# The zeros ahead of the attention's values: a DMA from a constant instead of GpSimd's memset

## The chip, the core and the metric

The kernel runs on one core of one Trainium2 chip. The metric is device time in microseconds (us) of one execution. The core's engines run side by side and meet at semaphores: PE (TensorE, matmuls), DVE (VectorE), ACT (ScalarE), POOL (GpSimd) and SP (SyncE, which only issues DMAs here). POOL and ACT can issue DMAs too.

## What is computed

A sequence of 2048 positions with 512 channels goes through four layers, each added to its input: a state-space convolution (A), a sliding dilated attention (B), then A and B again with the same weights. Cut to what matters:

```python
def _B_ref(x, wqkv, wo):
    H = 32; Dh = D // H
    W, dil = 8, 2
    q, k, v = qkv[0], qkv[1], qkv[2]          # of x @ wqkv
    idx = pos[:, None] - off[None, :]         # off = arange(W) * dil
    mask = idx >= 0
    vg = v[:, :, idx_c, :].reshape(B, H, S, W, Dh)
    logits = jnp.where(mask[None, None, :, :], logits, -1e9)
    attn = _softmax(logits, axis=-1)
    o = jnp.einsum("bhsw,bhswd->bhsd", attn, vg)
    return (lambda x, *d: x.transpose(*d))(o, 0, 2, 1, 3).reshape(B, S, D) @ wo

x = A_u
x = x + _A_ref(_layernorm(x, axis=-1), ...)   # y = causal convolution with a kernel made of A, B, C, dt
x = x + _B_ref(_layernorm(x, axis=-1), B_wqkv, B_wo)
x = x + _A_ref(_layernorm(x, axis=-1), ...)
x = x + _B_ref(_layernorm(x, axis=-1), B_wqkv, B_wo)
```

Each position looks at itself and at the seven positions 2, 4, ... 14 before it. The first positions would look ahead of the sequence's start; there the mask takes the weight away.

## The kernel before

**Layout.** Position 16 p + j lies in partition p at place j, so a partition holds 16 neighbouring positions (`NJ = 16`), and the activations `X` stay in SBUF as 128 partitions × 16 places × 512 channels, in two halves of 256.

**The tile VX.** The attention's values lie in `VX`, of 128 partitions × 2 halves × 30 places × 256 channels in bf16. Places 14 to 29 (`NV = 14`) are the partition's own positions, written by ACT (line 1485). Places 0 to 13 are the 14 positions before them, which belong to the partition one below; the function `shift` copies them there by DMAs of SP from partitions 0 to 126 to partitions 1 to 127 (line 1498). For partition 0 there is nothing to copy: its places 0 to 13, which head the sequence, must hold zeros, so that the products of line 1695 multiply the masked weights with numbers. They are written once, ahead of the first attention layer, and stay for the second.

**The order of the work.** Within a layer the code only declares operations, each with an engine: `pl.op("G", ...)` is for POOL, "V" for DVE, "A" for ACT, "P" for PE and "S" for SP. A written-out list of numbers for each layer (`ORDERS`) sets the order in which they are recorded, and each engine runs its instructions in that order, one after the other. Semaphores are put in by what an instruction reads and writes. So an instruction that stands still holds up all that follow it on its engine, whatever those read.

Constants for the later layers are loaded by POOL's own DMA queue just before the first attention layer; the zeros follow on the same engine:

```python
for name, arr, dt in (("IC2", _bf(C["IC2"]), BF), ("minus", _bf(-np.eye(128)), BF), ("down", np.eye(128, k=1, dtype=np.float32), F32)):
    C[name] = load_const(nc, const2, name, arr, dt, nc.gpsimd)
```

**What runs beside it.** POOL comes to these lines while the other engines are still in the last quarter of the first convolution, in `kernel_and_first_conv`. The channels come in four groups (`dc`), each in four parts. For a part of the kernel's spectrum, PE transposes a stage `Z` (tile `pt`, line 908), DVE copies it to SBUF (`zt`, line 912; other parts go by a transposing DMA of SP, line 885), PE multiplies it (`xp`, line 892) and ACT casts the result (`sp_k`, line 903), which SP also stores to HBM (line 951). For the input's spectrum `sp_u` the two halves of the partitions are also needed swapped; this is done by two DVE copies of 64 partitions each (line 959):

```python
for h in range(2):
    move(box["U"][64 * h:64 * h + 64, t], box["U"][64 - 64 * h:128 - 64 * h, s])
```

DVE then multiplies the spectra (`pa`, line 967), PE transforms back (`vp`, line 981), ACT or DVE casts that to SBUF (`VT`, line 984), and PE forms the output and adds the input (`ps_y`, lines 1000 and 1003), which ACT casts into `X` (line 1007). PE's results lie in three PSUM buffers of one ring (`psA`), used in turn. Then the attention layer begins: PE transposes `X` (`pt_x`, line 1301) and projects it (`ps_qk`, lines 1420 and 1439; `ps_v`, line 1474). DVE multiplies queries with keys (`prod`, line 1519), which PE sums into logits (`Lp`, line 1530).

Of the kernel before, what the change touches and what calls it, by code (L numbers as in the profile page):

```python
# [17 lines left out]
NPBF = ml_dtypes.bfloat16  # L18
# [14 lines left out]
NV = 14  # L33
# [1219 lines left out]
def b_layer(nc, tc, C, X, Wt, VX, XT, pst, eps, ln, center, evac, done, VSTAT_Q):  # L1253

    with ExitStack() as es:
# [19 lines left out]
        pl = Plan(psA=2, psL=1, psO=2, prod=4, LT=3, sm1=1, sm2=1, sm_m=1, sm_s=1, rdb=1)  # L1275
        turned, Kd, Qd, Kx, Vd, Ld, Sd, Od, Rs, Wd, Wl = {}, {}, {}, {}, {}, {}, {}, {}, {}, {}, {}
# [7 lines left out]
        def fetch(name):  # L1284
            if name == "wo":
                for ft in range(4):
                    nc.sync.dma_start(wo_t[:, ft, :], Wt["osrc"][ft])
            else:
                nc.sync.dma_start(bones[:], Wt["bsrc"])
# [523 lines left out]
            done(pl, qt, es)  # L1813

        if center:
            Wl["VX"] = pl.op("G", 1.0, lambda: nc.gpsimd.memset(VX[0:1, :, 0:NV], 0.0))
            for name, us in (("bones", 0.4), ("wo", 2.5)):
                Wl[name] = pl.op("S", us, lambda name=name: fetch(name), lag=5.0)
            for name in "kqv":
                Wd[name] = pl.outer(("w", name))  # L1820
# [39 lines left out]
def kernel(  # L1860
# [38 lines left out]
    with tc.tile_pool(name="mid", bufs=1) as mid:  # L1899
# [38 lines left out]
        def stored(pl, q, after):  # L1938
            for j, a in enumerate(after, q * 4):
                pl.op("S", 0.45, lambda j=j: nc.sync.dma_start(ov[:, j, :].rearrange("p (h c) -> p h c", h=2), X[:, :, j, :]), a, lag=2.2)  # L1940
        b_layer(nc, tc, C, X, Wt, VX, turned_view(U), pst, eps, ln, True, summed, normed, BN_Q)
        a_layer(nc, tc, C, X, kt_dram, U)
        b_layer(nc, tc, C, X, Wt, VX, turned_view(U), pst, eps, ln, False, lambda j, ps: nc.scalar.copy(X[:, :, j, :], halves(ps)), stored, range(4))


# [28 lines left out]
```

## Time and profile before

| | |
|---|---|
| three runs | 439.0, 437.52 and 435.03 us, median 437.52 |
| the profiled execution | 438.79 us, its span 437.0 |
| mean granted clock of PE in it | 0.960 |
| busy in the span | DVE 408.2 us, PE 376.1, ACT 321.1, POOL 33.5 |
| DMA | 51.48 MB, 118 GB/s on average |

The span runs from the first to the last instruction of the profiled execution, and all times of its rows count from the span's start. The granted clock is the share of PE's full clock that the chip's throttle let through. A row that names a line gives an engine's start and duration there; in square brackets stands how long the engine had been idle before it, and what released it. The chain that ended last is followed back from the last instruction: at each step to what released it, or to the instruction before it on its engine.

### The profile page before, as it was taken

To read this page: it belongs to the slowest core of one execution; us is meant where nothing else is said; L and a number is where in the kernel's file an instruction comes from. 1 tells how busy PE (TensorE), PEld (TensorE's weight loads), DVE (VectorE), ACT (ScalarE), POOL (GpSimd) and SP (SyncE) were. 2 spreads that over 40 slices of the span, in tenths; PEclk is the share of its full clock that TensorE was granted. 3 is DMA by queue.
4 is the path that set the end of the run, shared out by engine and by line. 5 is a ranking of instruction groups with operands and counts; after the bars stand their busy time and mean duration, and the time that the engine had idled before them with its cause. 6 is when DMAs were issued, how large, how long until landed. Compare 5 with 4: busy or idle time off the path is not lost.

```text
span 437.0 us, 11576 instructions
## 1 busy us (share of the span) xinstructions
PE 376.1 (86%) x4797; PEld 238.0 (54%) x4834; DVE 408.2 (93%) x682; ACT 321.1 (73%) x524; POOL 33.5 (8%) x97
## 2 busy tenths in 40 slices
PE   1278868898998678999999799899999999998995
PEld 1153646776887565446654345578774346743452
DVE  6999999998999977999899999999999899999994
ACT  6999989998998545667943568999966578853431
POOL 1000000000000700000100240020000010000150
PEclk9757989998999969999999999999999999999999
DMA  8996266777987628000322399089973000223295
GB/s 226 209 281 239 82 97 140 152 154 167 169 140 138 149 67 172 14 18 20 86 85 48 74 232 185 17 152 212 182 125 33 37 1 2 85 83 72 43 157 163
DMA packets 102171, 51.48 MB, mean 118 GB/s; under 512 B 81821, under 2 KB 93998, under 8 KB 101862
## 3 DMA queue, kind: packets, MB, share of 16 engines
q1 hardware_dynamic: 98758, 45.24, 48.4%
q0 software_dynamic: 3072, 5.23, 6.1%
q8 instruction: 38, 0.62, 0.6%
q10 hardware_dynamic: 288, 0.26, 0.2%
q14 instruction: 15, 0.12, 0.1%
HBM read 19.29 MB, written 6.29 MB: 59 GB/s over the span
## 4 chain that ended last, share of the span: by engine, by line
PE 49%; DVE 18%; ACT 10%; issue 4%; DMA 1%; SPq 0%; DVEq 0%; ACTq 0%
PE po L1711 7%; PE ps_v L1474 6%; PE ps_qk L1420 6%; PE ps_qk L1439 6%; DVE prod L1695 5%; PE ps_o L1795 4%; PE Lp L1530 4%; PE ps_s L872 3%; DVE prod L1519 2%; PE psk L483 2%; DVE sp_u L959 2%; PE ps_s L1117 2%; PE vp L981 1%; PE vp L1183 1%; ACT X L1209 1%
## 5 line engine op out<-in xcount | busy, mean ns | idle before, releaser
L1695 DVE TENSOR_TENSOR prod<-VX,L 128x512 bf16<-128x512 bf16 (+2 forms) x72 | 75.4, 1099 | 1.8 <-ACT VX L1485 1.0
L1519 DVE TENSOR_TENSOR prod<-qT,kT 128x4096 bf16<-128x4096 bf16 (+1 forms) x40 | 72.1, 1859 | 2.2 <-ACT kT L1462 1.0
L1711 PE MATMUL po<-prod,sb_ident 128*128 128x512 bf16 x233 | 56.4, 379 | 2.8 <-DVE prod L1695 2.0
L1711 PEld LDWEIGHTS <-sb_ident 128*128 128x128 bf16 x240 | 23.1, 97 | 31.3 <-issue 4.1
L875 ACT CAST Z<-ps_s 128x1024 bf16<-128x1024 f32 (+1 forms) x36 | 31.9, 929 | 1.7 <-PE ps_s L872 1.6
L1474 PE MATMUL ps_v<-wv,U 128*128 128x256 bf16 x256 | 31.4, 273 | 0.6 <-ACT VX L1485 0.3
L1795 PE MATMUL ps_o<-wo_t,oT 128*128 128x512 bf16 x124 | 31.3, 379 | 0.3 <-ACT oT L1744 0.2
L1420 PE MATMUL ps_qk<-U,wqk 128*128 128x512 bf16 x128 | 30.7, 380 | 0.3 <-ACT L L1658 0.3
L1485 ACT ACTIVATE VX<-ps_v,rs 128x256 bf16<-128x256 f32 x64 | 26.7, 473 | 5.6 <-PE ps_v L1474 5.1
L1729 ACT CAST ot<-po 128x1024 bf16<-128x1024 f32 (+1 forms) x16 | 15.1, 958 | 21.2 <-PE po L1711 21.2
L1439 PE MATMUL ps_qk<-U,wqk 128*128 128x512 bf16 x128 | 29.3, 379 | 0.0
L1474 PEld LDWEIGHTS <-U 128*128 128x128 bf16 x256 | 24.3, 97 | 8.9 <-issue 3.1
L1530 PE MATMUL Lp<-prod,sb_bones 128*32 128x512 bf16 x256 | 22.9, 383 | 3.0 <-DVE prod L1519 2.9
L892 PE MATMUL xp<-zt,sb_C 128*128 128x512 bf16 x45 | 16.1, 407 | 8.7 <-DVE zt L912 4.6
L967 DVE TENSOR_TENSOR pa<-sp_u,sp_k 128x2048 bf16<-128x2048 bf16 x16 | 19.4, 1220 | 3.7 <-PE vp L981 2.0
L1359 DVE BATCH_NORM_STATS2 pst<-X 128x6 f32<-128x256 bf16 x64 | 21.8, 407 | 0.5 <-ACT X L1209 0.5
L903 ACT CAST sp_k<-xp 128x1024 bf16<-128x1024 f32 x16 | 16.5, 1041 | 6.9 <-PE xp L892 6.3
L1420 PEld LDWEIGHTS <-wqk 128*128 128x128 bf16 x128 | 11.8, 98 | 16.8 <-issue 3.6
L1439 PEld LDWEIGHTS <-wqk 128*128 128x128 bf16 x128 | 12.2, 98 | 15.4 <-issue 1.6
L1795 PEld LDWEIGHTS <-oT 128*128 128x128 bf16 x128 | 12.2, 98 | 14.7 <-ACT oT L1744 0.7
L872 PE MATMUL ps_s<-KT,FK 128*128 128x128 bf16 (+1 forms) x360 | 18.8, 209 | 1.6 <-ACT KT L845 0.7
L1171 DVE TENSOR_TENSOR pa<-xc,Kt 128x2048 bf16<-128x2048 bf16 x16 | 18.9, 1218 | 0.6 <-PE vp L1183 0.3
(230 smaller groups left out, 863.1 us busy)
## 6 DMA issues: line engine op xcount, KB each, us to landing
kt_scratch<-sp_k SPq DMA_DIRECT2D x16, 256.0 KB, 2.7
Kt<-kt_scratch POOLq DMA_DIRECT2D x16, 256.0 KB, 6.7
sp_u<-sp_u SPq DMA_DIRECT2D x18, 128.0 KB, 2.6
X<-in_A_u_dram SPq DMA_DIRECT2D x8, 256.0 KB, 5.3
X<-in_A_u_dram SPq DMA_DIRECT2D x4, 512.0 KB, 5.3
Kt<-kt_scratch SPq DMA_DIRECT2D x8, 256.0 KB, 5.1
out_dram<-X SPq DMA_DIRECT2D x16, 128.0 KB, 2.0
VX<-VX SPq DMA_DIRECT2D x4, 448.0 KB, 3.7
```

Of the source, the lines that this page charges most:

```text
L872: nc.tensor.matmul(ps[:, r, 0:n // 4, jj * 4:(jj + 1) * 4], w, x, start=(k == 0), stop=(k == len(todo) - 1))
L875: nc.scalar.copy(box["Z", kind, dc, b0][:, 0:n // 4, :, jq * 16:(jq + 1) * 16].rearrange("p g r k -> p r g k"), box.pop(("s1", kind, dc, j ...
L1359: nc.vector.bn_stats(pst[:, j, cp, :], X[:, cp, j, :])
L1420: nc.tensor.matmul(ps[:], wqk[:, ct, f0:f0 + 128], XT[:, ct // 2, 4 * s:4 * s + 4, ct % 2, :], start=(ct == 0), stop=(ct == 3))
L1439: nc.tensor.matmul(box[name][:, k * 512:k * 512 + 512], wqk[:, ct, f0:f0 + 128], XT[:, ct // 2, 4 * s:4 * s + 4, ct % 2, :], start=(ct == ...
L1474: nc.tensor.matmul(ps[:, jj].rearrange("p t h d -> p (t h d)"), XT[:, ct // 2, j + jj, ct % 2, :], wv[:, ct, fp * 256:(fp + 1) * 256], sta ...
L1485: nc.scalar.activation(out, ps, ACT.Identity, scale=r)
L1519: nc.vector.tensor_tensor(pr[:], windows(q, 0, 2), windows(kT[fp][:, a:a + n2, col(w):col(w) + 1024], -DIL * 128, 2), ALU.mult)
L1530: nc.tensor.matmul(Lp[r0:r0 + 32, w // 4, :], bones[:, w % 4 + k, :], pr[:, k, f2 - a, hb * 512:(hb + 1) * 512], start=(n == 1 and k == 0) ...
L1695: nc.vector.tensor_tensor(p2[:].rearrange("p w j t d h -> p w (j t) d h"), windows(v, -DIL * 256, taps), l.to_broadcast([128, taps, nj * 2 ...
L1711: nc.tensor.matmul(po[:, c:c + 512], ident[:], p2[:, t, k + j:k + j + 2].rearrange("p j t d h -> p (j t d h)"), start=first, stop=stop)
L1795: nc.tensor.matmul(ps, oT[:, ft // 2, o:o + 128], wo_t[:, ft, :], start=(ft == 0 and not res), stop=(ft == 3))
```

## The change

POOL no longer writes the zeros itself. They stand in HBM as a constant of the program, and POOL issues a DMA that copies them to the same place, partition 0, places 0 to 13 of both halves, 14336 bytes in two runs of 7168:

```diff
         if center:
-            Wl["VX"] = pl.op("G", 1.0, lambda: nc.gpsimd.memset(VX[0:1, :, 0:NV], 0.0))
+            zeros = nc.inline_tensor(np.zeros((1, 2, NV, 256), NPBF), name="c_zeros")
+            Wl["VX"] = pl.op("G", 1.0, lambda: nc.gpsimd.dma_start(VX[0:1, :, 0:NV], zeros.ap()))
```

`center` is true in the first attention layer only. No instruction changes its place. On POOL, between the constants' loads and the first zeros of the softmax's tiles (`RR`):

```order
 L127 DMA sb_minus<-c_minus 128x128
 L127 DMA sb_down<-c_down 128x128
-L1816 MEMSET VX 1x2x3584
+L1817 DMA VX<-c_zeros 1x2x3584
 L1392 MEMSET RR 1x16
 L1392 MEMSET RR 1x32
```

One row has become a DMA. As it takes one of the eight semaphores on which GpSimd's DMAs are counted in turn, each later one moves to the next. On DVE the first product that reads VX, in the first attention layer, gets one wait more (DMASW5, the zeros' own), with the waits of each instruction in brackets:

```order
 L1644 TENSOR_TENSOR L_4014<-L_4014,sm_m 128x1024 [waits DVE_49]
 L1664 TENSOR_TENSOR L_4014<-L_4014,sm_rdb 128x1024 [waits PE_49,Activation_49]
-L1695 TENSOR_TENSOR prod_4629<-VX,L_4014 128x4096 [waits DMAHW5_49,DMAHW6_49,DVE_49,Activation_49]
+L1695 TENSOR_TENSOR prod_4629<-VX,L_4014 128x4096 [waits DMAHW5_49,DMASW5_49,DMAHW6_49,DVE_49,Activation_49]
 L1695 TENSOR_TENSOR prod_4631<-VX,L_4014 128x4096
```

With the memset no such wait stood there; other waits of the program imply its order. Nothing else on DVE moves but line numbers and semaphore numbers.

## The prediction

> **What bounds the kernel now.** I began with the busy shares, then asked for the one instruction that the change touches and for its neighbours on GpSimd (POOL) in order of time.
>
> ```profile
> PE 376.1 (86%) x4797; PEld 238.0 (54%) x4834; DVE 408.2 (93%) x682; ACT 321.1 (73%) x524; POOL 33.5 (8%) x97
> ```
>
> POOL is busy for 8% of the span, so a shorter POOL instruction is worth nothing by itself.
>
> ```profile
> 146.17 0.54 POOL L127 DMA_DIRECT2D sb_down<-c_down  x1
> 146.69 6.27 POOL L1816 MEMSET VX<- 1x7168 bf16 x1
> 189.06 0.93 POOL L1392 MEMSET RR<- 1x16 bf16 x10 [36.10 <-ACT RR L1386]
> ```
>
> The columns are start, duration, engine, line and operation. The memset runs from 146.69 to 152.96 us, and POOL then idles 36.10 us on ScalarE (ACT): nothing on its own queue waits for it. So I looked at what the other engines did meanwhile, in the list of the copies of line 959 and in the chain that ended last.
>
> ```profile
> L959 DVE COPY sp_u<-sp_u x14: 419/422/6276, 74.0 to 156.4; 64x1024 bf16<-64x1024 bf16 x14
> ```
>
> ```profile
> 146.50 0.45 DVE sp_u L959
> 146.96 0.01 issue
> 146.97 6.28 DVE sp_u L959
> ...
> 154.15 0.70 DVE zt L912
> ...
> 158.49 1.71 PE vp L981 x16
> 160.19 0.45 PE xp L892 x2
> ...
> 161.72 1.24 DVE pa L967
> ...
> 163.00 1.08 PE vp L981 x16
> ...
> 165.77 0.21 PE ps_y L1000
> 165.99 0.45 PE ps_y L1003 x8
> ```
>
> Fourteen VectorE (DVE) copies have one shape and a median of 0.422 us; one took 6.276 us. It starts at 146.97, just inside the memset, and ends at 153.25, 0.29 us after it. The copy is on the chain, and TensorE (PE) sits behind it:
>
> ```profile
> 149.49 0.61 PE L908 MATMUL pt<-sb_ident,Z 128*128 128x128 bf16 x8
> 149.94 0.38 PE L892 MATMUL xp<-zt,sb_C 128*128 128x512 bf16 x1
> 154.90 1.03 PE L892 MATMUL xp<-zt,sb_C 128*128 128x512 bf16 x2 [4.58 <-DVE zt L912]
> ```
>
> PE idles 4.58 us for the copy zt, which stands in DVE's queue behind the blocked one. Here **VectorE, held up by the memset, sets the pace**, not DVE's own work. The stretches of the granted clock (PE busy, then PEclk, DMA share and GB/s) show a second cost:
>
> ```profile
> 98.64:102.06 3.42, 1.72 (x18) 1.00 1.07 200
> 102.06:105.47 3.41, 3.25 (x25) 0.50 0.52 137
> 149.84:153.26 3.42, 0.48 (x6) 1.00 0.62 153
> 153.26:156.67 3.41, 1.77 (x8) 0.50 0.00 0
> 156.67:160.08 3.41, 3.41 (x32) 0.50 0.23 82
> ```
>
> After the stretch with PE busy 0.48 of 3.42 us, its clock is at 0.50 for the next two, to 160.08, so the chain's PE work runs at half speed just when it has to catch up.
>
> **The change part by part.** *Removed:* the memset's 6.27 us on POOL, which covers nothing. With it goes the wait of one copy, 6.28 − 0.42 = 5.86 us of DVE time, so the copies ahead of zt, which now starts at 154.15, would be done at 148.3. *What is late next:* zt copies what PE's eight transposes wrote, done at 149.49 + 0.61 = 150.10. So zt starts at 150.13, not then: 4.02 us earlier than 154.15. The other 1.84 us become idle time of DVE. The matmuls on zt follow 0.75 us after its start, as now (154.15 to 154.90), at 150.88. They also need ACT's cast X, since it frees their PSUM buffer:
>
> ```profile
> 149.69 1.01 ACT L1007 CAST X<-ps_y 128x1024 bf16<-128x1024 f32 x1 [0.59 <-PE ps_y L1003]
> 150.61 1.01 ACT L903 CAST sp_k<-xp 128x1024 bf16<-128x1024 f32 x1
> ```
>
> It ends at 150.70, just in time. PE's idle time falls from 4.58 to some 0.5 us, PE is busy for 0.48 + (153.26 − 150.88) = 2.86 us of the stretch that had 0.48, and its clock should stay at 1.00.
>
> *The half clock:* from 154.90 PE works without a break through xp, two ps_y, vp and another xp, 5.74 us to 160.19 + 0.45. At full clock a 512-column matmul takes 0.21 and eight of L1003 0.45 (rows 165.77 and 165.99), sixteen of vp half of 1.71: 0.43 + 1.32 + 0.86 + 0.43 = 3.04 us. That would be 2.7 us more, if PE alone set the pace; so I follow the other engines: DVE's rows behind zt, and the transposed tile that the last xp reads:
>
> ```profile
> 154.75 1.22 DVE L967 TENSOR_TENSOR pa<-sp_u,sp_k 128x2048 bf16<-128x2048 bf16 x1
> 156.00 0.86 DVE L959 COPY sp_u<-sp_u 64x1024 bf16<-64x1024 bf16 x2
> 157.01 1.22 DVE L967 TENSOR_TENSOR pa<-sp_u,sp_k 128x2048 bf16<-128x2048 bf16 x1
> ```
>
> ```profile
> 149.12 1.24 SPq L885 DMA_TRANSPOSE zt<-Z  x1
> ```
>
> ```profile
> zt<-Z SPq DMA_TRANSPOSE x1, 3.1
> ```
>
> - First pa 0.60 after zt's start (as 154.15 to 154.75), 150.73 to 151.95; PE's vp would start at 150.88 + 0.43 + 1.32 = 152.63, so pa is ready.
> - The last xp 0.86 later at 153.49; its tile lands at 149.12 + 3.1 = 152.2, ready.
> - Two copies 1.25 after pa's start (154.75 to 156.00), 151.98 to 152.84. ACT's sp_k follows the one at 150.61 by 0.92, as that follows X, and ends at 152.54. So the second pa starts at 152.87 (157.01 before) and ends at 154.09; its vp takes 154.12 to 155.2.
> - The third pa waits for the first vp and then runs from 154.0. The fourth waits for the second vp, for ACT's sp_k of the last xp (154.1 to 155.1) and for DVE: it starts at 155.2, against 161.72: **6.5 us earlier**.
> - The vp behind it starts at 156.5 in place of 163.00: again 6.5.
>
> From there, every next step waits for this chain (X, its transposes, the projections), the waits between the instructions are the old ones, and everything moves as a block. *Added:* one DMA issue on POOL at 146.69, by sb_down's row 0.54 us. The row before it is the test of what an issue does to a copy: the copy at 146.50 ran beside sb_down's issue in 0.45 us. The bounds are nothing and, if it held a copy for its whole time, 0.54; even then the copies end by 148.8, before 150.10, so I take **0**. Its landing: 14 KB; the nearest row is 16 KB,
>
> ```profile
> sb_block<-c_block POOLq DMA_DIRECT2D x1, 16.0 KB, 3.8
> ```
>
> so at about 150.5 us. The added wait for it stands at the first product that reads VX:
>
> ```profile
> 215.84 4.49 DVE L1695 TENSOR_TENSOR prod<-VX,L 128x4096 bf16<-128x4096 bf16 x2 [1.01 <-ACT VX L1485]
> ```
>
> This would come at 209.3; behind it stand DVE's further products and PE's sums, but the cover is over 58 us. The semaphores of GpSimd's later DMAs shift by one; what these waits name now was issued before the zeros, or is the zeros, far ahead in the program: 0.
>
> Sum: **−6.5 us on the profiled execution**, whose own time is 438.79 (437.0 span and 1.8 around it): 432.3. How long the half clock lasts hangs on where the 3.41 us stretches fall. Here it lasted 160.08 − 154.90 = 5.2 us into the work, since the stretch with 1.77 us of work didn't end it; placed otherwise, it could end up to one stretch sooner, after 1.8. The loss of 6.5 − 4.0 = 2.5 us would then be 0.9, and this execution is above the median. With 4.0 and the middle, 1.7 (an estimate), the median gains 5.7: 437.52 − 5.7 = **431.8**.
>
> The row of the blocked copy, 0.29 us past the memset's end, bears on a rule: the Trainium skill, "SBUF — State Buffer", "Who interferes with whom", has VectorE's two-port copies and GpSimd instructions share one port pair, which the first to issue keeps to its end. The trace agrees. The same section speaks against this change: descriptors of a GpSimd DMA are written through that pair and starve beside such copies. By that the issue would wait till 148.3 at most, the sum would stay, and the row of 0.45 us shows no copy hurt by one.
>
> **The rivals.** *The clock drops all the same.* PE would have to be half idle between 150 and 157. Against it: the pieces above leave PE little idle time; for it, the stretch 98.64 to 102.06 shows that half idle is enough. Then the gain is zt's 4.0 alone: 433.5.
>
> *The drop comes elsewhere.* The whole program behind 163 us slides against the stretches.
>
> ```profile
> 239.16:242.57 3.41, 1.22 (x11) 1.00 0.16 31
> 242.57:245.98 3.41, 2.33 (x32) 1.00 0.25 46
> ```
>
> A stretch that fell on 239.16 to 242.57 would hold 1.22 us of PE work, less than the 1.72 that sufficed at 98.64. The next 2.33 us of work would double: at most +2.3, so 434.1. The kernel before carries the same risk in other executions, hence a small chance. The Trainium skill, "TensorE: Matmul & The Clock Gate", Part 1 (The HAM clock gate), gives the half clock after an idle window of about 3.4 us; by that alone, no drop could come here, and the row of 98.64 differs, which is why I keep this rival.
>
> *The change doesn't free the copy*, because something other than the memset held it: 437.5. The matching ends and the median of 0.422 us speak against it.
>
> *Slower: the zeros go as single elements.* If the DMA were split into 7168 packets,
>
> ```profile
> q1 hardware_dynamic: 98758, 45.24, 48.4%
> ```
>
> at this queue's 0.484 × 16 × 437.0 / 98758 = 0.034 us each, that is 246 us of one DMA engine. On two engines (VX has two rows here) it lands at 147 + 123 = 270, 61 us after 209.3: some 492. It decides as soon as the landing takes over 62 us, with fewer than four engines. Against it: both sides are two runs of 7168 contiguous bytes.
>
> **How the numbers follow.** Main case 0.80; the clock drops all the same 0.06; elsewhere 0.06; copy not freed 0.04; slower 0.04. A 1% change, about what a measurement of this kernel tells from none, is 4.4 us: faster below 433.1. The main case's runs reach from 435.03 − 5.7 = 429.3 to 439.00 − 5.7 = 433.3, so I put 0.08 of its 0.80 within 1%, with the first three rivals: 0.72, 0.24, 0.04. The range goes from the fastest run with the full gain, 435.03 − 6.5 = 428.5, to the slowest with the least, 439.00 − 4.0 = 435.0, which takes in both clock rivals.
>
> **What would show it.** All fourteen copies of line 959 near 0.42 us; zt right behind the last transposes, near 150.1; PE's wait for it under 1 us; a clock of 1.00 from 150 to 165; vp, now 163.00, near 156.5; the first product on VX 6.5 us earlier and released by ACT, not by the zeros. Wrong would be: a copy as long as before beside the DMA's issue, the clock at 0.50 again, or a gain at 163 us that is gone at the end.

## The result and the profile after

Six runs of the changed kernel took 429.95 to 432.12 us, median **430.52**; six of the kernel before, on the same chip, 435.03 to 439.61, median 438.13. The ratio is **0.9844 (95% interval 0.9803 to 0.9886)**, a gain of 1.6%, by the ratio 6.8 us (5.0 to 8.6). Forecast were 431.8 us and a range of 428.5 to 435.0: faster, by the way described, and a little too cautious. (One run of `pieces` below, 495.43 us with a mean clock of 0.746, and one of before beside it, 462.44 us with 0.858, were slow through the whole program and stand in no ratio, so that the profile of `pieces` is read from the same kernel's run `pieces2`.)

The profiled execution took 430.11 us, its span is 428.3 (438.79 and 437.0 before). First the busy times and the granted clock by slices, from the page of the kernel after:

```profile
PE 370.3 (86%) x4797; PEld 233.4 (54%) x4834; DVE 402.2 (94%) x682; ACT 320.9 (75%) x524; POOL 27.7 (6%) x97
...
PEclk9999999999999999999999999999999999999999
```

and the clock's line from the page of before:

```profile
PEclk9757989998999969999999999999999999999999
```

DVE is busy for 6.0 us less (408.2 before), nearly all of it the one blocked copy. PE is busy for 5.8 us less, though its instructions are the same 4797: it ran at full clock throughout, where before shows four dips: two in the first 60 us, one near 103 us and one near 155. Only the last lies where the change is. Keep this apart; it explains why the profiles differ by more than the change is worth.

Now the place of the change, after. POOL in order of time (start, duration, engine, line and operation):

```profile
143.78 0.54 POOL L127 DMA_DIRECT2D sb_down<-c_down  x1
144.30 0.53 POOL L1817 DMA_DIRECT2D VX<-c_zeros  x1
```

The list of line 959 (least, median and greatest duration in ns):

```profile
L959 DVE COPY sp_u<-sp_u x14: 420/422/502, 73.9 to 150.0; 64x1024 bf16<-64x1024 bf16 x14
```

DVE and then PE in order of time:

```profile
143.25 2.70 DVE L959 COPY sp_u<-sp_u 64x1024 bf16<-64x1024 bf16 x6
147.75 0.69 DVE L912 COPY zt<-pt 128x1024 bf16<-128x1024 bf16 x1 [1.80 <-PE pt L908]
...
150.57 3.67 DVE L967 TENSOR_TENSOR pa<-sp_u,sp_k 128x2048 bf16<-128x2048 bf16 x3
```

```profile
147.10 0.61 PE L908 MATMUL pt<-sb_ident,Z 128*128 128x128 bf16 x8
...
148.50 0.61 PE L892 MATMUL xp<-zt,sb_C 128*128 128x512 bf16 x2 [0.57 <-DVE zt L912]
...
154.30 1.07 PE L981 MATMUL vp<-sb_IC,pa 128*128 128x128 bf16 x16 [0.24 <-DVE pa L967]
```

No copy takes longer than 0.502 us, and DVE now idles 1.80 us until PE's transposes are done: the roles are turned round, and DVE waits for PE. PE's own wait for zt is 0.57 us in place of 4.58. Its clock from there, in one stretch (PE busy, PEclk, DMA share, GB/s):

```profile
150.00:165.00 15.00, 12.88 (x145) 1.00 0.76 171
```

**Where the time came from.** Compare starts, before and after, along the program. sb_down's issue on POOL, ahead of the change, already comes 2.39 us earlier (146.17 to 143.78). That is the early clock, and the change has no part in it. At 42 us PE's rows of the two still agree within 0.04 (42.27 and 42.23, line 1022); behind before's half-clock stretch of 57.69 to 61.10 they are 1.35 apart (62.51 and 61.16, line 838), and behind that of 102.06 to 105.47, 2.39 (105.63 and 103.24, line 483). Before's other executions vary in this too, with mean clocks of 0.960 to 0.994. zt comes 6.40 earlier (154.15 to 147.75), 4.01 more. The fourth pa starts at 153.01, against 161.72: 8.71 earlier, 2.31 more. From there it stays: the first product on VX is 8.70 earlier (215.84 to 207.14), and so is the span's end. So the change is worth 4.01 + 2.31 = **6.3 us** in this pair of profiles, and the early clock the other 2.4.

### The profile page after: what moved, and what is told of

Read it like the earlier page. It is cut to its first block, busy times and chain, and to the rows that moved or that the text cites. A ratio compares the mean times of both kernels' runs of the same rounds, so it can differ in the third digit from the quotient of the medians.

```text
span 428.3 us, 11576 instructions
## 1 busy us (share of the span) xinstructions
PE 370.3 (86%) x4797; PEld 233.4 (54%) x4834; DVE 402.2 (94%) x682; ACT 320.9 (75%) x524; POOL 27.7 (6%) x97
## 3 DMA queue, kind: packets, MB, share of 16 engines
q0 software_dynamic: 3104, 5.24, 6.1%
## 4 chain that ended last, share of the span: by engine, by line
PE 48%; DVE 15%; ACT 14%; issue 4%; DMA 1%; ACTq 0%; DVEq 0%
PE po L1711 8%; PE ps_v L1474 7%; PE ps_qk L1420 7%; PE ps_qk L1439 6%; DVE prod L1695 5%; PE ps_o L1795 4%; PE Lp L1530 4%; PE psk L483 3%; DVE prod L1519 3%; ACT Z L875 2%; DVE pa L967 2%; PE ps_s L1117 2%; PE ps_s L872 1%; ACT sp_k L903 1%; PE vp L1183 1%
## 5 line engine op out<-in xcount | busy, mean ns | idle before, releaser
L892 PE MATMUL xp<-zt,sb_C 128*128 128x512 bf16 x45 | 15.0, 380 | 5.0 <-ACT zt L912 2.3
L872 PEld LDWEIGHTS <-FK 128*128 128x128 bf16 x360 | 17.4, 98 | 3.2 <-issue 2.3
```

The source lines that it names most:

```text
L872: nc.tensor.matmul(ps[:, r, 0:n // 4, jj * 4:(jj + 1) * 4], w, x, start=(k == 0), stop=(k == len(todo) - 1))
```

## The experiments

The theory: (1) the copy is held for exactly as long as GpSimd's memset runs; (2) that delays zt, with PE behind it; (3) the idle time halves PE's clock for the catching up, which costs some 2 us more; (4) the DMA that replaces the memset is free. Each run attacks one of these. Undo, half, pieces and later share the runs of before on one chip (median 437.42); warm, double and pieces2 those on another (436.55). In the table, in us and read from each kernel's own profile, the second column is the time that the six copies of line 959 ahead of zt take together, the third runs from the start of the first of them to zt's start, the fifth from zt's start to that of the fourth pa behind it.

| kernel | the six copies | to zt | PE's wait for zt | zt to fourth pa | ratio to before |
|---|---|---|---|---|---|
| before | 8.48 | 8.51 | 4.58 | 7.57 | 1 |
| after | 2.70 | 4.50 | 0.57 | 5.26 | 0.9844 (0.9803–0.9886) |
| undo | 8.48 | 8.51 | 4.58 | 6.72 | 0.9999 (0.9974–1.0024) |
| half | 5.49 | 5.53 | 1.59 | 5.26 | 0.9879 (0.9838–0.9921) |
| pieces2 | 3.55 | 4.50 | 0.35 | 5.89 | pieces: 0.9864 (0.9819–0.9909) |
| later | 2.62 | 4.51 | 0.57 | 5.26 | 0.9849 (0.9806–0.9891) |
| warm | 8.48 | 8.51 | 0.91, fillers ahead | 5.27 | 0.9949 (0.9930–0.9968) |
| double | 14.34 | 14.36 | 10.22 | 6.53 | 1.0147 (1.0119–1.0175) |

**undo: the DMA stays, a memset of the old size comes back** ahead of it, on places that line 1498 fills later anyway (against after):

```diff
+ nc.gpsimd.memset(VX[32:33, :, 0:NV], 0.0)
  nc.gpsimd.dma_start(VX[0:1, :, 0:NV], zeros.ap())
```

> The changed kernel, with a GpSimd memset of the same size put back ahead of the zeros' DMA; it writes 7168 zeros to partition 32 of VX, which the shift DMAs overwrite later, so the computation is the reference's. Theory A (a memset on GpSimd holds a VectorE copy for as long as it runs): one copy of line 959 takes about 6.3 us and ends some 0.3 us after the memset, TensorE waits about 4.6 us for zt, its clock drops for 3.4 to 6.8 us, and the time is that of the kernel before, 438 (436 to 440). Rival B (what cost the time was how VX's zeros are waited for, not the memset's run): all copies at 0.42, about 430.5. Rival C (the difference was luck with the clock in the first 100 us): no copy held, any time between 430 and 438.

Measured in 10 runs: 437.33 us against 437.42. POOL, the copies and DVE in its profile:

```profile
145.10 6.22 POOL L1818 MEMSET VX<- 1x7168 bf16 x1
```

```profile
L959 DVE COPY sp_u<-sp_u x14: 420/422/6277, 74.0 to 154.8; 64x1024 bf16<-64x1024 bf16 x14
```

```profile
152.50 0.69 DVE L912 COPY zt<-pt 128x1024 bf16<-128x1024 bf16 x1
```

The memset alone brings back the long copy and the whole loss; the constant and the DMA cost nothing that ten runs can show. That the memset was on the path, and not something else gone with it, rests on this run.

**half: a memset of half the length, the DMA for the other half** (against after):

```diff
- nc.gpsimd.dma_start(VX[0:1, :, 0:NV], zeros.ap())
+ nc.gpsimd.memset(VX[0:1, 0:1, 0:NV], 0.0)
+ nc.gpsimd.dma_start(VX[0:1, 1:2, 0:NV], zeros.ap()[:, 1:2])
```

> Half of the zeros by memset (3584 elements, issued first), the other half by DMA; the computation is the reference's. The memset should take 3.1 us. Theory A with my slack and clock terms: one copy takes about 3.2 us, the copies ahead of zt end about 2.8 us later than in the changed kernel, of which 1.8 us are slack behind TensorE's transposes, so zt is 0.9 to 1.0 us late, TensorE waits about 1.5 us and its clock doesn't drop: about 1 us over the changed kernel, 431.5. Rival D (the cost goes with the memset's length, since each microsecond of held VectorE counts): half of the gain, 434.

Measured: 432.45 us (431.76 to 433.06). POOL, the copies and PE:

```profile
145.66 3.28 POOL L1818 MEMSET VX<- 1x3584 bf16 x1
```

```profile
L959 DVE COPY sp_u<-sp_u x14: 421/422/3289, 74.0 to 152.4; 64x1024 bf16<-64x1024 bf16 x14
```

```profile
150.88 0.60 PE L892 MATMUL xp<-zt,sb_C 128*128 128x512 bf16 x2 [1.59 <-DVE zt L912]
```

The longest copy shrinks with the memset: 3.289 us beside 3.28. This separates delay from damage: the copies lose 2.8 us, but zt comes only 1.03 us later, since 1.80 us of DVE's idle time takes the rest. PE's wait grows by the same 1.02 us, and its two matmuls take 0.60 us in place of 1.03: the clock did not drop. Half of the memset costs far less than half of the loss, because the slack is eaten first and the clock stays up. (The times alone, 0.9879 beside 0.9844, don't separate half from after; the trace does. Expected were 431.5 us, and the median lies 0.95 above: by the ratios half is some 1.5 us slower than after, by the trace 1.0.)

**pieces, and pieces2 for its profile: the same zeros by fourteen memsets of 512** (against before):

```diff
- nc.gpsimd.memset(VX[0:1, :, 0:NV], 0.0)
+ for k in range(NV):
+     nc.gpsimd.memset(VX[0:1, :, k:k + 1], 0.0)
```

> The kernel before, with its memset cut into 14 of 512 elements each, back to back; the computation is the reference's. The same elements are written by the same engine. Theory A, if the hold is taken anew by each instruction: a copy waits for one memset of about 0.5 us at a time, so the copies and memsets alternate, none of the copies takes over about 1 us, the copies ahead of zt are late by 1.5 to 2.5 us, which the slack of 1.8 us takes up, and the time is 430 to 431.5. Rival E (GpSimd keeps what it holds until its queue is empty): one copy of about 7 us again, 438.

> The kernel before with the memset in 14 pieces once more, for an undisturbed profile. Theory A: no copy over about 1 us, zt within 1 us of the end of the transposes, the clock at 1.00 there; rival E: one copy of about 7 us.

Measured: `pieces` 430.85, 431.87 and 432.8 us; `pieces2` 433.13, one run. POOL, the copies and DVE of pieces2:

```profile
146.83 8.17 POOL L1818 MEMSET VX<- 1x512 bf16 x14
```

```profile
L1818 POOL MEMSET VX<- x14: 515/516/798, 146.8 to 154.5; 1x512 bf16 x14
```

```profile
L959 DVE COPY sp_u<-sp_u x14: 420/424/737, 74.1 to 152.9; 64x1024 bf16<-64x1024 bf16 x14
```

```profile
150.27 0.69 DVE L912 COPY zt<-pt 128x1024 bf16<-128x1024 bf16 x1 [0.95 <-PE pt L908]
...
152.13 1.48 DVE L959 COPY sp_u<-sp_u 64x1024 bf16<-64x1024 bf16 x2
```

POOL works for longer in all, 8.17 us, yet no copy takes over 0.737: a copy waits for the memset that is running, not for POOL's queue to run dry. The six copies lose 0.85 us in the slack; the two later ones lose 0.62 us, and the fourth pa comes that much later behind zt (5.89 beside 5.26). Expected were 430 to 431.5 us with the copies 1.5 to 2.5 us late; the three runs have a median of 431.87, and the expectation had no term for the two later copies. zt, which reads PSUM, and the first pa ran beside the pieces in their usual 0.69 and 1.22 us. It is not POOL's work that counts, but the length of one instruction.

**later: the whole memset, moved** to where POOL next writes zeros, some 37 us on, beside DVE's products (against before; the operation at the old place does nothing):

```diff
  # ones(), behind the memsets of RR
+ if center:
+     nc.gpsimd.memset(VX[0:1, :, 0:NV], 0.0)
```

> The kernel before, with its one memset recorded after the first zeros of RR, so that it runs some 40 us later, at about 190 us, beside VectorE's products of line 1519 (two inputs in SBUF) and one cast from PSUM; the computation is the reference's. Theory A, if only the copies of line 959 with one input in SBUF are held: the products keep their 1.2 and 2.2 us, the memset ends before the next GpSimd work, and the time is that of the changed kernel, 430.5 (429.5 to 432). Rival F (any VectorE instruction on SBUF is held): one product takes about 6 us longer, and 434 to 438. Rival B: slower than the changed kernel with nothing held.

Measured: 431.16 us (429.88 to 432.52). POOL and DVE of later:

```profile
181.56 6.06 POOL L1394 MEMSET VX<- 1x7168 bf16 x1
```

```profile
182.17 1.22 DVE L1446 CAST qT<-ps_qk 128x1024 bf16<-128x1024 f32 x1
183.52 8.90 DVE L1521 TENSOR_TENSOR prod<-qT,kT 128x4096 bf16<-128x4096 bf16 x4
```

and the same products after, with nothing beside them:

```profile
183.19 8.90 DVE L1519 TENSOR_TENSOR prod<-qT,kT 128x4096 bf16<-128x4096 bf16 x4
```

The same 6 us of memset cost nothing here: cast and products last as long as without it, and the ratio is that of the DMA. So it was never the memset's length alone, but what DVE does beside it. The Trainium skill, "SBUF — State Buffer", "Who interferes with whom", says which instructions can collide: VectorE's copies can take the port pair that GpSimd uses, an instruction with two SBUF inputs contends only with a GpSimd instruction that reads, and one with a single input outside the two-port modes not at all. Copies held, products and the cast from PSUM untouched: the trace agrees. The ports themselves no run shows.

**warm: the memset stays, sixteen matmuls that nobody reads fill PE's wait** (against before, ahead of the xp that waits):

```diff
+ if (kind, dc, i) == ("k", 3, 2):
+     fill = psK.tile([128, 512], F32, name="fill", tag="psk")
+     for _ in range(16):
+         nc.tensor.matmul(fill[:], ident[:], F1T[:, 0:2].rearrange("p j r c -> p (j r c)"), start=True, stop=True)
```

> The kernel before, memset and all, with 16 matmuls of 512 columns added on TensorE ahead of the pair that waits for zt; they go to a PSUM tile that nobody reads, so the computation is the reference's. They last about 3.4 us of the 4.6 us for which TensorE waits. Theory A with its clock term: the copy is still held for 6.3 us and zt comes no sooner, but the clock stays at 1.00, the fourth pa follows zt by 5.3 us as in the changed kernel (7.6 before, 6.7 with the memset put back), and the time falls by the clock's part alone, 1.4 to 2.3 us: 435.5 (434.5 to 436.3). Rival H (the half clock costs nothing here because other engines set the pace): 437.4, and the pa 6.7 to 7.6 us behind zt.

Measured in 12 runs: 434.51 us against 436.55, by the ratio 2.2 us (1.4 to 3.1) faster. PE and DVE of warm, and the clock by stretches (PE busy, PEclk, DMA share, GB/s):

```profile
148.65 3.62 PE L892 MATMUL fill<-sb_F1T,sb_ident 128*128 128x512 bf16 x16
153.17 0.60 PE L896 MATMUL xp<-zt,sb_C 128*128 128x512 bf16 x2 [0.91 <-DVE zt L916]
```

```profile
152.42 0.69 DVE L916 COPY zt<-pt 128x1024 bf16<-128x1024 bf16 x1
```

```profile
153.10:156.50 3.40, 3.25 (x38) 1.00 0.21 77
156.50:159.90 3.40, 3.06 (x48) 1.00 0.50 128
235.70:239.09 3.39, 1.20 (x17) 1.00 0.34 65
239.09:242.50 3.41, 2.86 (x28) 0.50 0.06 12
```

This takes the clock's part by itself. zt is as late as before (8.51 us behind the first copy), but the clock stays at 1.00 and zt to the fourth pa takes 5.27 us, as after. The rival by which the fillers gain nothing, 437.4, falls. The last two rows are a find: the prediction's rival of a drop elsewhere did come about here, behind a stretch with 1.20 us of PE work. It cost nothing that shows: warm's fourth pa starts 4.0 us ahead of before's (157.69 for 161.72), and its span is still 4.3 us shorter; some 1.7 us of both is the early clock, by sb_down's issue (144.45 for 146.17).

**double: a second memset behind the first** (against before):

```diff
  nc.gpsimd.memset(VX[0:1, :, 0:NV], 0.0)
+ nc.gpsimd.memset(VX[32:33, :, 0:NV], 0.0)
```

> The kernel before with a second memset of the same size right behind the first, on partition 32 of VX, where the shift DMAs write later; the computation is the reference's. Theory A: two copies of line 959 are held, each for about 6.2 us (or one for 12.5), zt is a further 6.2 us late, all of it on the path, since the slack of 1.8 us is used up by the first: 443.6 (443 to 445). Rival I (the second memset has to wait until VectorE's queue of copies is done): one held copy and 437.4. Rival B: 437.4.

Measured: 442.9 us, 6.35 over before's 436.55 (by the ratio 5.2 to 7.6). POOL, DVE and PE of double:

```profile
146.43 6.27 POOL L1817 MEMSET VX<- 1x7168 bf16 x1
152.75 6.24 POOL L1818 MEMSET VX<- 1x7168 bf16 x1
```

```profile
145.37 14.34 DVE L959 COPY sp_u<-sp_u 64x1024 bf16<-64x1024 bf16 x6
```

```profile
146.70 6.28 DVE sp_u L959
...
152.99 6.28 DVE sp_u L959
```

```profile
160.48 1.03 PE L892 MATMUL xp<-zt,sb_C 128*128 128x512 bf16 x2 [10.22 <-DVE zt L912]
```

Two copies are held, one by each memset, so the rival by which the second memset waits for the copies falls. With no, one and two memsets the six copies take 2.70, 8.48 and 14.34 us: 5.78, then 5.86 a memset, against the 5.86 of the prediction (and in later, with neither memset nor DMA beside them, 2.62). Expected were 443.6 us (443 to 445); the median of 442.9 misses that narrowly, but before is 436.55 on this chip, and the 6.35 over it fit the expected 6.2. The second memset costs about what the first did, but the price is made up otherwise: its full length at zt (14.36 for 8.51 us), with no slack left to take any of it, and nothing more by the clock, which was down already (6.53 us from zt to the fourth pa, 7.57 before). In this pair of profiles, counted from sb_down's issue (145.90 for 146.17), the fourth pa is only 4.8 us later than before's, less than the runs' interval: before's profiled execution took 1.0 us more from zt to the fourth pa, at the half clock.

## Why the prediction was right

- **The copy is freed, 5.86 us.** Right: greatest duration 0.502 us after, and the steps of double.
- **zt 4.02 us earlier, 1.84 of slack.** Right: 4.01, and DVE idles 1.80. Half shows the slack from the other side.
- **PE's wait some 0.5 us, no half clock.** Right: 0.57 us, 1.00 from 150 to 165.
- **6.5 us at the fourth pa.** Measured 6.3. The prediction had the fourth pa 5.07 us after zt; it is 5.26. The second pa is 0.08 later than worked out, and the third, which the prediction released by PE, follows in DVE's own queue. The chain of waits after shows it, without zt and with the products on it end to end:

```profile
150.57 2.37 DVE pa L967 x2
152.94 0.03 DVEq L967
152.97 0.04 issue
153.01 1.24 DVE pa L967
```

- **The half clock's loss, 2.5 us in that execution and 1.7 in the middle.** Measured 2.3 in that execution (7.57 less 5.26), 1.5 in undo, where the clock was back at 157.69, and 2.2 (1.4 to 3.1) by warm's runs. So the middle was a little low, some 0.5 us of the 1.3 by which 431.8 lies above 430.52; the rest, 0.8, is less than before's medians vary from one set of runs to the next (436.55 to 438.13), so its cause stays open. The interval of the gain, 5.0 to 8.6, holds 5.7, 6.3 and 6.5 alike.
- **The DMA costs nothing.** Right, and the landing was overestimated: 2.1 us, not 3.8. The list of line 1817:

```profile
L1817 POOL DMA_DIRECT2D VX<-c_zeros x1: 527/527/527, 144.3 to 144.3; - x1
...
DMA to landing us min/median/max: 2.1/2.1/2.1
```

The starvation of such a DMA beside copies, which the Trainium skill states ("SBUF — State Buffer", "Who interferes with whom"), does not show here: it was issued while the copies ran, in 0.53 us, and the slowest of the copies, the one of 0.502 us, lost 0.08 at most to the median. Nor did it split into elements, the slower rival: GpSimd's queue carries 32 packets more, 3104 for 3072, not 7168. The first product on VX is still released by ACT:

```profile
207.14 4.49 DVE L1695 TENSOR_TENSOR prod<-VX,L 128x4096 bf16<-128x4096 bf16 x2 [1.01 <-ACT VX L1485]
```

- **What the prediction didn't see:** that two executions differ by 2.4 us ahead of the change through the early clock. After's runs with a mean clock of 0.999 took 429.95 to 430.22 us, those of 0.967 to 0.972 took 430.82 to 432.12. It used before's spread for the range, which covered this. How many of six runs start slow was not forecast: the median of after's three fast starters is 430.11, of the others 431.85, so the distance of 430.52 from 431.8 is in part chance.

## What to carry to other kernels

An engine that is busy for 8% can still set the pace: look in the list of one line for the single instruction that is far above its group's median, and for what runs beside it on GpSimd. A long GpSimd memset beside VectorE copies within SBUF can be moved to where VectorE multiplies or reads PSUM (as good as a DMA here), or cut into pieces; other GpSimd instructions were not tried. Its price is its length, less the slack of what waits, plus the clock that PE loses while it is starved. To tell these apart, change the length by half and by double, and fill PE's wait with idle matmuls.

## What was unexpected of the hardware

- A memset of one partition's 7168 elements takes 6.27 us, of 3584 3.28, of 512 0.516 by the median of the fourteen: nearly in proportion to the elements. It holds a copy of 64 partitions by 1024 that needs 0.42 us alone, on partition 0 as on 32.
- The holding goes both ways. In pieces2 six of the fourteen pieces were issued while a copy ran, and these six took 0.72 to 0.80 us in place of 0.52; the whole memset, issued while a copy ran, took 6.27 us, and in later, beside products, 6.06.
- The clock needs no idle stretch to halve. Of the stretches ahead of a drop, PE was busy 0.48 and 1.72 us of 3.42 (before), 1.03 of 3.41 (undo) and 1.20 of 3.39 (warm). In before, whose drops show where its stretches of 3.41 us lie, one with 1.75 was followed by 1.00 (from 74.75 to 78.17):

```profile
71.34:74.75 3.41, 1.75 (x20) 1.00 0.76 167
```

That does not fix a bound between 1.72 and 1.75: the ends of matmuls are modelled, and busy time is not all that counts. At half clock, a stretch with 3.07 us of 3.42 (23.55 to 26.97), in matmuls of 1 and 32 columns, was not followed by full clock.
- Sixteen matmuls that nobody reads, with the memset left in place, bought a third of the change's gain (2.2 us of 6.8).
